# A clustered-attention and SiLU kernel: the hand-written opening list reordered, loads of later batches issued at other steps, output quarters placed in other PSUM banks

## The chip, the core and the metric

The kernel runs on one core of a Trainium2 chip. A core has five engines with queues of their own: TensorE (PE, with its weight loads shown as PEld), VectorE (DVE), ScalarE (ACT), GpSimd (POOL) and SyncE (SP), which here only issues DMAs. An engine takes its queue strictly in the order in which the program lists it. TensorE writes into PSUM, of which this kernel uses eight banks: four single ones, numbered 0 to 3, and two pairs for the scores. The metric is the device time of one execution in microseconds, as the median of several runs.

## The reference

```python
q_n, k_n, c_n = ...                      # each row divided by its norm
q_assign = np.argmax(np.einsum('bhsd,hcd->bhsc', q_n, c_n), axis=-1)
k_assign = np.argmax(np.einsum('bhsd,hcd->bhsc', k_n, c_n), axis=-1)
mask = q_assign[:, :, :, None] == k_assign[:, :, None, :]
scores = np.where(mask, scale * np.matmul(q, k.transpose(0, 1, 3, 2)), -1000000000.0)
attn = ...                               # softmax over the keys
x = np.matmul(attn, v)                   # (4, 8, 768, 64), then to (3072, 512)
h = x @ w_in                             # (3072, 2048)
out = (h * (1.0 / (1.0 + np.exp(-h)))) @ w_out
```

There are 4 batches of 8 heads, 768 rows, 64 columns per head and 16 clusters per head. All inputs and the output are 32-bit floats; the kernel computes with half-precision operands.

## The kernel before

**Tiles.** A job is the rows of one head: 768 keys and 768 queries as twelve blocks of 128 rows (for batch 0 a job `k0` to `k7` holds six key blocks and the first three query blocks of a head; two jobs `x0` and `x1` hold the second halves of the queries of four heads each). The rows arrive in a `raw` tile (eight buffers). They are split into a high and a low half-precision part: `hi` (line 105) multiplies and rounds, on ACT, GpSimd or VectorE, and `lo` (line 117) subtracts on VectorE; both write the tile `hl` (four buffers). A transpose brings them into `ab`: in the opening on TensorE (`tr`, line 134) with an eviction by VectorE or ACT (`ev`, line 146), in the later batches by a transposing DMA (`xpose`). From `ab` TensorE computes the cluster logits (`logits_n`); VectorE takes their maximum (`mx_n`) and compares (`ge_n`), and the one-hot rows so found are turned by TensorE (`cd_mm`, or `ct_mm` for two early jobs), scaled (`cd_ev`) and brought into `ab` by a small DMA on SP. With them in the contracted dimension, the product of queries and keys holds the mask.

**Scores and values.** `units` lists 192 steps: for each batch, half of the queries, group of four heads and head, three pairs of key blocks. A step is two score matmuls (`qk_mm`, line 303, into one of two pairs of banks) and one exponential on ACT (`exp`, line 316). Six steps give two heads; then `pv` (line 324) multiplies with the values, `norm` divides, and the result goes transposed into `xt`, by TensorE (`xn_t`, `xn_ev`) or by DMA (`xn_d`). Values are loaded by SP (`load_v`, line 253, five buffers) and cast by GpSimd (`cast_v`, line 258).

**The two dense layers.** When all heads of a batch half stand in `xt`, sixteen up-projections `unit_a` (four matmuls each, then a tanh on ACT and a product on VectorE) fill `gt`; then three row blocks of the output follow, each of four quarters `part_b` (line 425, four matmuls of 512 columns). A row block collects in one PSUM bank, which VectorE evicts (line 437) and SP stores. Batch halves follow one another; while the steps of one are computed, the dense layers of the one before fill TensorE.

**Weights.** `w_load` (line 443) issues, on GpSimd's queue, eight loads of w_in (0 to 7) and four of w_out (8 to 11); the latter are held back by a small copy that waits for an exponential.

**The opening** runs up to step 24 in an order written out by hand, the string `plan` (line 602). Each word is one operation of `first` (line 521): `hi2.P` is the split of job 2 on GpSimd; `xh0`, `xl0` are `hi`, `lo` of job `x0`; `xp0`, `xq0` its two transposes, `xu0`, `xw0` their evictions, `xL0`, `xM0` its logits, `xm0`, `xg0`, `xc0`, `xe0` the steps to its one-hot rows. `qk9`, `ex9` are the scores and the exponential of step 9; `ce3` evicts the one-hot rows of job 3 and issues the DMA that I call `cd3`. `pa1`, `pb1`, `pc1` are the three thirds of the value product of the second pair of heads, `px3`, `py3` the two heads of the last pair; `nm`, `pt`, `pe` normalise, transpose and evict. `a0`, `e0` begin and end an up-projection (three matmuls and the last one); `w0` to `w9` are weight loads, `vl`, `v` a value load and its cast; `j2` are two filler matmuls and `fill(11)` at the start eleven. A digit behind a dot names the PSUM bank.

**After the opening** a loop runs over the steps from 24 on. `at` holds what a step does beside its scores: `put` places the loads, splits, transposes and logits of job i around a step p, which is 32, 35, 39, ... for batch 1 and five steps apart later (made odd). `take` (line 661) fills TensorE: each step adds 1.46 of credit less its own cost, and as long as credit is positive it takes the next `unit_a` (0.66) or `part_b` (0.87). A quarter may be taken only while `gap` is positive and, until a new batch half is five steps away, only while more than five quarters are left (`HOLD`). The three banks 0 to 2 go round in a list `free`; each user takes the first and returns it when its eviction is listed. Bank 3 serves the output quarters.

Of the kernel before, what the change touches and what calls it, by code (L numbers as in the profile page):

```python
# [28 lines left out]
def kernel(  # L29
# [11 lines left out]
    B, H, S, D = q.shape  # L41
# [21 lines left out]
    free, where = [0, 1, 2], {}  # L63
# [214 lines left out]
    jobs = {}  # L278
# [11 lines left out]
    for i in range(H, B * H):  # L290
        h = i % H
# [165 lines left out]
    def fill(n, bk=3):  # L457
        if n:
            junk = bank("junk", n=bk)
            for _ in range(n):  # L460
                nc.tensor.matmul(junk, zz[:, 0:128], zz, start=True, stop=True)
# [10 lines left out]
    nc.vector.memset(ones, 1.0)  # L472
    for vt in vtb:
        nc.vector.memset(vt[:, :, D : D + 1], 1.0)
    fill(11)
    nc.gpsimd.memset(hf, 0.5)
    chl = mp.tile([128, 4, D], f16, name="chl")
    nc.gpsimd.memset(chl[:, 3, :], 0.0)
# [42 lines left out]
    def first(op, n, eng, banks):  # L521
        job = jobs.get(n)
        xj = jobs["x", n] if n < 2 else None
        if op == "j":
            fill(n, banks[0])
        elif op == "hi":
            for part in (K, Qp) if n == 0 else (None,):
                hi(job, {"A": "act", "P": "pool", "D": None}[eng], part)
        elif op == "lo":
            for part in (K, Qp) if n == 0 else (None,):  # L530
                lo(job, part=part)
        elif op == "tr":
            tr(job, banks)
        elif op in ("evk", "evq"):
            ev(job, op[2], eng)
        elif op == "L":
            logits_n(job, banks[0])
        elif op == "mx":
            mx_n(job)
        elif op == "ge":  # L540
            ge_n(job)
        elif op == "cm":
            cd_mm(job)
        elif op == "ce":
            cd_ev(job, eng)
        elif op == "ct":
            ct_mm(job, banks)
        elif op == "ctq":
            ct_q(job)
        elif op == "ctk":  # L550
            ct_k(job)
        elif op == "qk":
            qk_mm(n)
        elif op == "ex":
            exp(n)
        elif op == "vl":
            load_v(n)
        elif op == "v":
            cast_v(n)
        elif op == "w":  # L560
            w_load(n, {8: 22, 9: 23}.get(n))
        elif op in ("pa", "pb", "pc"):
            t = "abc".index(op[1])
            pv(2 * n, 0, banks and banks[0], [(t, 0), (t, 1)])
        elif op in ("px", "py"):
            pv(2 * n, 0, banks and banks[0], [(t, "xy".index(op[1])) for t in range(NM)])
        elif op == "a":
            begun[n] = unit_a_begin(0, 0, n)
        elif op == "e":
            unit_a_end(0, 0, n, begun.pop(n) if n in begun else unit_a_begin(0, 0, n))()  # L570
        elif op == "nm":
            norm(2 * n, 0)
        elif op == "pt":
            xn_t(2 * n, 0, banks[0])
        elif op == "pe":
            xn_ev(2 * n, 0, eng)
        elif op == "xr":
            load(xj)
        elif op == "xh":
            hi(xj, {"P": "pool", "D": None}[eng])  # L580
        elif op == "xl":
            lo(xj)
        elif op == "xt":
            xpose(xj)
        elif op in ("xp", "xq"):
            tr(xj, banks, "k" if op == "xp" else "q")
        elif op in ("xu", "xw"):
            ev(xj, "k" if op == "xu" else "q", eng)
        elif op in ("xL", "xM"):
            logits_n(xj, banks and banks[0], ns=range(6) if op == "xL" else range(6, 12))  # L590
        elif op == "xm":
            mx_n(xj)
        elif op == "xg":
            ge_n(xj)
        elif op == "xc":
            cd_mm(xj)
        elif op == "xe":
            cd_ev(xj, eng)
        else:
            raise ValueError(op)  # L600

    plan = """
        hi0.A lo0 tr0.32 hi2.P j2.1 evk0.D evq0.A c5.01 j2.2 stk hi1.A L0.3 lo2 j1.2 kad xr0
        mx0 tr2.02 hi3.P ge0 j1.1 lo1 j1.1 evk2.A evq2.D ct0.10 hi4.P lo3 vl1 vl0 xr1 L2.2 ctq0 ctk0 tr1.31 mx2 hi5.P
        qk0 evk1.D evq1.A vl2 ex0 tr3.01 ge2 lo4 cm2 hi6.P L1.3 evk3.A ce2.D qk1 vl4 evq3.A mx1 tr4.02 ex1 ge1
        L3.1 hi7.P evk4.D evq4.A qk2 mx3 ct1.02 ex2 ge3 v1 lo5 cm3 ctq1 L4.3 v0 ce3.A ctk1 w0 tr5.01 mx4 v2
        qk3 ge4 evk5.A w1 evq5.D qk4 lo6 cm4 ex3 j2.2 ce4.D vl3 ex4 v4 qk5 lo7 L5.2 ex5 qk6 mx5 tr6.10 ex6 ge5 qk7
        xh0.P evk6.D cm5 ex7 qk8 ce5.D tr7.31 evq6.D ex8 qk9 evk7.D L6.2 vl5 ex9 w2 evq7.D qk10 mx6 v3 L7.0 ex10
        ge6 qk11 cm6 ex11 pa0.3 ce6.D pb0 mx7 qk12 w3 ge7 ex12 v5 qk13 pc0 cm7 ex13 nm0 ce7.D qk14 ex14 xl0 xh1.P qk15 xp0.1 pt0.3 qk16 pe0.D xu0.D xq0.2 xw0.D
        ex15 vl6 w4 ex16 qk17 pa1.0 vl7 xL0.2 qk18 pb1 ex17 w5 xM0 xm0 xg0 qk19 pc1 xc0 ex18 nm1 xe0.D qk20 w6 v6 pa2.1 ex19  # L610
        pt1.0 qk21 pb2 ex20 pe1.D xl1 w7 v7 qk22 pc2 xp1.2 ex21 nm2 xu1.D qk23 xq1.0 px3.3 ex22 pt2.1 xw1.D ex23 w8 pe2.D xL1.2 xM1 xm1 xg1 a0 py3 nm3 xc1 a1 w9 pt3.3 pe3.D xe1.D e0 e1 qk24 ex24 e2
    """.split()
    for word in plan:
        name, *rest = word.split(".")
# [8 lines left out]
        else:  # L623
            op = name.rstrip("0123456789")
# [5 lines left out]
    def put(s, f, *a):  # L630
        at.setdefault(s, []).append((f, a))
# [3 lines left out]
    for i in range(H, B * H):  # L635
        b, h = divmod(i, H)
        p = int((32 + 3.5 * h, 64 + 5 * h, 104 + 5 * h)[b - 1]) | 1
        job = jobs[i]
        e = 1 if b == 1 else 2
        put(p - 8 - 2 * (b > 1), load, job)  # L640
        put(p - 6, load_v, i)
        put(p - 3 * e, hi, job)
        put(p - 1 - e, lo, job)
        put(p - e, xpose, job)
        put(p, cast_v, i)
        put(p + 5, logits_1, job)
        put(p + 5, lsum, job)
        put(p + 5, mx_n, job)
        put(p + 5, ge_n, job)
        put(p + 7, cd_mm, job)  # L650
        put(p + 7, cd_ev, job, "D")
# [3 lines left out]
    qa, qb = [(0, 0, fb) for fb in range(3, NFB)], []  # L655
# [5 lines left out]
    def take(hold, held):  # L661
        nonlocal turn, gap
        b_ok = len(qb) > hold and gap > 0
        if qa and not (b_ok and (held or turn >= 4)):
            turn = (turn + 1) % 7
            gap += 1
            it = qa.pop(0)
            while not free:
                late.pop(0)()
            late.append(unit_a(*it))  # L670
            if it[2] == NFB - 1:
                qb.extend((it[0], it[1], t, n) for t in range(NM) for n in range(4))
            return 0.66
        if b_ok:
            turn = (turn + 1) % 7
            f = part_b(*qb.pop(0))
            if f:
                late.append(f)
                gap = -1
            return 0.87  # L680
        return 0.0

# [135 lines left out]
```

## Time and profile before

| what | value |
|---|---|
| median of 3 runs | 324.86 us (323.74 to 325.95) |
| profiled execution | 326.72 us, of which the span is 324.9 us |
| mean granted TensorE clock | 0.989 |
| HBM read and written | 27.30 MB and 6.29 MB |
| largest groups on TensorE | up-projection 91.2 us, scores 92.2 us, output 89.2 us, value product 41.5 us |
| exponentials on ACT | 192 of 811 ns, 152.6 us |

The span is the time from the first to the last instruction of one profiled execution; the rest of that execution lies around it. A group's busy time adds up its instructions; matmuls overlap in the pipeline, so the groups' sum is larger than the time that TensorE was busy. In a row of the timeline stand the start, the duration, the engine, the line and the operation, the tile written and the tiles read, shapes and count, and in brackets how long the engine stood idle before and what released it.

### The profile page before, as it was taken

Reading aid. Unit: us, or ns where it says so; the run is one execution under the profiler, and the core shown is the slowest. Engines: PE = TensorE matmul, PEld = TensorE weight load, DVE = VectorE, ACT = ScalarE, POOL = GpSimd, SP = SyncE. Lnnn points to the kernel's source line nnn. Section 1 sums busy time; section 2 is a strip of 40 time slices with the busy share of each in tenths; the row PEclk is TensorE's granted clock in tenths of the full one; section 3 lists DMA queues with packets and bytes.
Section 4 is the critical chain, followed back from the end, with each engine's and each line's share of the span. In section 5 each row is a group of like instructions: output and inputs, shape, how many; then the busy total and the mean of one; then the engine's idle time right before and its main releaser. Section 6 shows DMA issues by size and latency. Waiting matters only on the chain.

```text
span 324.9 us, 7844 instructions
## 1 busy us (share of the span) xinstructions
PE 307.2 (95%) x3173; PEld 191.3 (59%) x3173; DVE 211.7 (65%) x445; ACT 209.4 (64%) x332; POOL 41.0 (13%) x68
## 2 busy tenths in 40 slices
PE   6997999997989999999999999999999999999995
PEld 2665765655556555665566656666566556655644
DVE  5897566779778655987598857893456315632641
ACT  2597649766468665885488656985589648961620
POOL 4884331101000000000010002000000000000000
PEclk9899899999999999999999999999999999999999
DMA  7756999999945686677887567853110111011001
GB/s 218 248 108 132 168 148 253 184 241 206 247 120 135 162 184 186 150 161 132 237 186 185 128 171 210 138 115 83 53 46 12 37 54 46 6 42 46 32 32 68
DMA packets 72613, 43.14 MB, mean 133 GB/s; under 512 B 50016, under 2 KB 68608, under 8 KB 72576
## 3 DMA queue, kind: packets, MB, share of 16 engines
q1 hardware_dynamic: 69024, 38.14, 47.3%
q0 software_dynamic: 3264, 4.20, 8.6%
q8 instruction: 25, 0.41, 0.5%
q10 hardware_dynamic: 288, 0.30, 0.3%
q14 instruction: 12, 0.10, 0.1%
HBM read 27.30 MB, written 6.29 MB: 103 GB/s over the span
## 4 chain that ended last, share of the span: by engine, by line
PE 74%; DVE 14%; ACT 3%; DMA 3%; issue 2%; SPq 2%; POOL 0%; DVEq 0%; ACTq 0%
PE po L430 23%; PE ph L380 20%; PE pS L313 13%; PE pO L330 9%; PE psN L168 3%; DVE hl L120 3%; DVE gt L400 2%; ACT tn L399 2%; DVE ot L437 2%; PE phs L410 2%; ACT P L318 2%; DVE mxn L193 2%; DMA ab<-hl 1%; PE po L782 1%; DVE L L180 1%
## 5 line engine op out<-in xcount | busy, mean ns | idle before, releaser
L318 ACT ACTIVATE P<-pS 128x768 f16<-128x768 f32 x192 | 152.6, 811 | 67.2 <-PE pS L313 67.0
L380 PE MATMUL ph<-xt,win_s 128*128 128x384 f16 x480 | 91.2, 326 | 3.2 <-DVE gt L400 1.7
L313 PE MATMUL pS<-ab 128*128 128x384 f16 x384 | 92.2, 328 | 0.7 <-ACT P L318 0.6
L430 PE MATMUL po<-wout_s,gt 128*128 128x512 f16 x368 | 89.2, 379 | 1.6 <-DVE ot L437 0.9
L400 DVE SCALAR_TENSOR_TENSOR gt<-tn,ph 128x384 f16<-128x384 f32 x120 | 64.0, 551 | 24.3 <-ACT tn L399 23.8
L399 ACT ACTIVATE tn<-ph 128x384 f32<-128x384 f32 x120 | 58.8, 496 | 15.9 <-PE ph L380 11.7
L380 PEld LDWEIGHTS <-win_s 128*128 128x128 f16 x480 | 45.8, 98 | 33.3 <-issue 4.7
L430 PEld LDWEIGHTS <-gt 128*128 128x128 f16 x368 | 34.5, 98 | 37.0 <-issue 3.4
L313 PEld LDWEIGHTS <-ab 128*128 128x128 f16 x384 | 34.7, 98 | 25.5 <-issue 1.7
L330 PEld LDWEIGHTS <-P 128*128 128x128 f16 x1152 | 40.3, 98 | 5.3 <-issue 0.7
L330 PE MATMUL pO<-vt,P 128*128 128x65 f16 x1152 | 41.5, 193 | 0.0
L260 POOL CAST vt<-vn 128x384 f16<-128x384 f32 x32 | 17.0, 533 | 157.5 <-DMA vn<-in_v_dram 127.5
L120 DVE SCALAR_TENSOR_TENSOR hl<-raw,hl 128x768 f16<-128x768 f32 (+3 forms) x35 | 33.9, 972 | 0.4 <-POOL hl L113 0.3
L437 DVE TENSOR_SCALAR ot<-po 128x512 f32<-128x512 f32 x23 | 15.8, 689 | 27.5 <-PE po L430 27.1
L168 PEld LDWEIGHTS <-ab 128*128 128x128 f16 x496 | 18.1, 98 | 5.6 <-DMA ab<-hl 1.5
L180 DVE TENSOR_REDUCE L<-psN 128x192 f32<-128x384 f32 x24 | 13.2, 552 | 11.9 <-PE psN L168 11.9
L168 PE MATMUL psN<-stk,ab 128*128 128x32 f16 (+1 forms) x496 | 19.3, 187 | 1.2 <-DMA ab<-hl 1.1
L342 DVE TENSOR_TENSOR xn<-pO,zr 128x384 f16<-128x384 f32 x32 | 17.8, 557 | 1.1
L340 DVE RECIPROCAL zr<-pO 128x6 f32<-128x6 f32 x32 | 6.2, 194 | 15.7 <-PE pO L330 15.7
L224 DVE TENSOR_SCALAR cd<-psC,kadd 96x256 f16<-96x256 f32 x24 | 11.4, 474 | 6.2 <-PE psC L211 6.0
L113 POOL TENSOR_SCALAR hl<-raw 128x576 f16<-128x576 f32 (+1 forms) x8 | 14.4, 1816 | 2.6 <-DMA raw<-in_q_dram 1.7
L115 DVE TENSOR_SCALAR hl<-raw 128x768 f16<-128x768 f32 x24 | 13.4, 560 | 2.0 <-DMA raw<-in_k_dram 1.9
(68 smaller groups left out, 138.8 us busy)
## 6 DMA issues: line engine op xcount, KB each, us to landing
vn<-in_v_dram SPq DMA_DIRECT2D x32, 192.0 KB, 3.1
raw<-in_k_dram SPq DMA_DIRECT2D x31, 192.0 KB, 3.3
out_dram<-ot SPq DMA_DIRECT2D x23, 256.0 KB, 2.3
raw<-in_q_dram SPq DMA_DIRECT2D x24, 192.0 KB, 2.8
win_s<-in_moe_w_in_dram POOLq DMA_DIRECT2D x8, 256.0 KB, 6.3
wout_s<-in_moe_w_out_dram POOLq DMA_DIRECT2D x4, 512.0 KB, 8.7
ab<-cd SPq DMA_DIRECT2D x26, 48.0 KB, 2.3
raw<-in_q_dram SPq DMA_DIRECT2D x2, 384.0 KB, 5.0
```

What stands on the lines that cost most here:

```text
L120: nc.vector.scalar_tensor_tensor(out=hl[:, s, 1, :], in0=raws[job.name][:, s, :], scalar=QS, in1=hl[:, s, 0, :], op0=ALU.mult, op1=ALU.sub ...
L168: nc.tensor.matmul(L[:, n % 2, :, n // 2], ab[:, i, :], stk[:, job.groups[i // 3][0], x : x + w], start=(x == 0), stop=(x + w == 2 * HC),)
L260: nc.gpsimd.tensor_copy(vt[:, :, 0:D], vns.pop(i))
L313: nc.tensor.matmul(pS[:, e, 0:HALF], abs_[kj.name][:, kn, :], rhs, start=True, stop=True)
L318: nc.scalar.activation(out=P, in_=pst.pop(u)[:, :, 0:HALF], func=AF.Exp, bias=0.0, scale=ESC)
L330: nc.tensor.matmul(o[:, (2 * t + h) * VW : (2 * t + h + 1) * VW], Ps[i + h, c, j // 2][:, j % 2, ts(t, 128)], vtb[(i + h) % 13][:, j, 0:VW ...
L342: nc.vector.tensor_tensor(out=xn, in0=ov[:, :, 0:D], in1=zr.unsqueeze(2).to_broadcast([128, 2 * NM, D]), op=ALU.mult)
L380: nc.tensor.matmul(ph[:, 0:HALF], win_s[:, r, ts(fb, 128)], xts[b, c][:, r, :], start=(r == 0), stop=(r == NR - 1))
L399: nc.scalar.activation(out=tn, in_=ph[:, 0:HALF], func=AF.Tanh, bias=0.0, scale=0.5)
L400: nc.vector.scalar_tensor_tensor(out=gt[:, fb, :], in0=tn, scalar=1.0, in1=ph[:, 0:HALF], op0=ALU.add, op1=ALU.mult)
L430: nc.tensor.matmul(po, gts[b, c][:, fc, ts(t, 128)], wout_s[:, fc, :], start=(fc == 0), stop=(fc == NFB - 1))
L437: nc.vector.tensor_scalar(out=ot, in0=po, scalar1=0.5, scalar2=None, op0=ALU.mult)
```

## The change

The change touches the opening list, the steps at which later loads are issued, and the bank and spacing of the output quarters. No instruction that computes is removed; two filler matmuls are added (`fill(13)`).

In the list, `w0`, `w1`, `w2` now stand right behind the splits `hi5`, `hi6`, `hi7` on GpSimd's queue and the other loads of w_in follow sooner. `vl3` and `vl5` are issued earlier on SP, each one `ce` sooner. `xl0` moves ahead of `ce7` and `nm0`; `xh1` is listed later, but on GpSimd's own queue it still follows the last load of w_in. `xp0` stands ahead of step 15's scores, `pt0` behind `xq0`. `py3` comes ahead of `xm1`, so `nm3` and `pt3` come sooner and `a0`, `a1` around them later. The rows of the first job of batch 1 (`r8`) are loaded inside the list.

In the loop, the rows of batch 1 are loaded 8 to 12 steps ahead of p (8 before), those of batches 2 and 3 16 steps ahead (10 before). When no up-projection is left, an output row block may start in any bank of `free`, and the quarters of the next one are not barred for two steps.

```diff
-    fill(11)
+    fill(13)
...
+        elif op == "r":
+            load(jobs[n])
...
-        mx0 tr2.02 hi3.P ge0 j1.1 lo1 j1.1 evk2.A evq2.D ct0.10 hi4.P lo3 vl1 vl0 xr1 L2.2 ctq0 ctk0 tr1.31 mx2 hi5.P
-        qk0 evk1.D evq1.A vl2 ex0 tr3.01 ge2 lo4 cm2 hi6.P L1.3 evk3.A ce2.D qk1 vl4 evq3.A mx1 tr4.02 ex1 ge1
-        L3.1 hi7.P evk4.D evq4.A qk2 mx3 ct1.02 ex2 ge3 v1 lo5 cm3 ctq1 L4.3 v0 ce3.A ctk1 w0 tr5.01 mx4 v2
-        qk3 ge4 evk5.A w1 evq5.D qk4 lo6 cm4 ex3 j2.2 ce4.D vl3 ex4 v4 qk5 lo7 L5.2 ex5 qk6 mx5 tr6.10 ex6 ge5 qk7
-        xh0.P evk6.D cm5 ex7 qk8 ce5.D tr7.31 evq6.D ex8 qk9 evk7.D L6.2 vl5 ex9 w2 evq7.D qk10 mx6 v3 L7.0 ex10
-        ge6 qk11 cm6 ex11 pa0.3 ce6.D pb0 mx7 qk12 w3 ge7 ex12 v5 qk13 pc0 cm7 ex13 nm0 ce7.D qk14 ex14 xl0 xh1.P qk15 xp0.1 pt0.3 qk16 pe0.D xu0.D xq0.2 xw0.D
-        ex15 vl6 w4 ex16 qk17 pa1.0 vl7 xL0.2 qk18 pb1 ex17 w5 xM0 xm0 xg0 qk19 pc1 xc0 ex18 nm1 xe0.D qk20 w6 v6 pa2.1 ex19
-        pt1.0 qk21 pb2 ex20 pe1.D xl1 w7 v7 qk22 pc2 xp1.2 ex21 nm2 xu1.D qk23 xq1.0 px3.3 ex22 pt2.1 xw1.D ex23 w8 pe2.D xL1.2 xM1 xm1 xg1 a0 py3 nm3 xc1 a1 w9 pt3.3 pe3.D xe1.D e0 e1 qk24 ex24 e2
+        mx0 tr2.02 hi3.P ge0 j1.1 lo1 j1.1 evk2.A evq2.D ct0.10 hi4.P lo3 vl1 vl0 xr1 L2.2 ctq0 ctk0 tr1.31 mx2 hi5.P w0
+        qk0 evk1.D evq1.A vl2 ex0 tr3.01 ge2 lo4 cm2 hi6.P w1 L1.3 evk3.A ce2.D qk1 vl4 evq3.A mx1 tr4.02 ex1 ge1
+        L3.1 hi7.P w2 evk4.D evq4.A qk2 mx3 ct1.02 ex2 ge3 v1 lo5 cm3 ctq1 L4.3 v0 w3 ce3.A ctk1 tr5.01 mx4 v2 vl3
+        qk3 ge4 evk5.A evq5.D qk4 lo6 cm4 w4 ex3 j2.2 ce4.D vl5 ex4 v4 qk5 lo7 L5.2 ex5 qk6 mx5 tr6.10 ex6 ge5 qk7
+        xh0.P w5 evk6.D cm5 ex7 qk8 ce5.D tr7.31 evq6.D ex8 qk9 evk7.D L6.2 v3 ex9 w6 evq7.D qk10 mx6 v5 L7.0 ex10
+        ge6 qk11 cm6 ex11 pa0.3 ce6.D pb0 mx7 qk12 w7 ge7 ex12 qk13 pc0 cm7 xl0 ex13 ce7.D vl6 vl7 r8 qk14 nm0 ex14 xp0.1 qk15 xu0.D xq0.2
+        ex15 qk16 xw0.D pt0.3 ex16 pa1.0 pe0.D qk17 xL0.2 ex17 xh1.P pb1 qk18 xM0 xm0 xg0 ex18 pc1 qk19 xc0 nm1 xe0.D v6 v7 ex19
+        pa2.1 qk20 pt1.0 pb2 ex20 pe1.D qk21 pc2 xl1 ex21 nm2 xp1.2 qk22 xu1.D ex22 xq1.0 px3.3 qk23 xw1.D pt2.1 pe2.D ex23 w8 xL1.2 xM1 py3
+        xm1 xg1 nm3 a0 xc1 pt3.3 a1 w9 pe3.D xe1.D e0 e1 qk24 ex24 e2
...
-        put(p - 8 - 2 * (b > 1), load, job)
+        if i > H:
+            put(p - (8 + min(h, 4) if b == 1 else 16), load, job)
...
-            f = part_b(*qb.pop(0))
+            f = part_b(*qb.pop(0), None if not qa and free else 3)
             if f:
                 late.append(f)
-                gap = -1
+                gap = -1 if qa else 1
```

## The prediction

> **What bounds the kernel now.** I read the engine totals of the page first, then busy time in windows, then the timeline wherever TensorE stands idle.
>
> ```profile
> span 324.9 us, 7844 instructions
> PE 307.2 (95%) x3173; PEld 191.3 (59%) x3173; DVE 211.7 (65%) x445; ACT 209.4 (64%) x332; POOL 41.0 (13%) x68
> 50.00:60.00 10.00, 10.00 (x92) 6.30 (x90) 7.70 (x15) 9.11 (x18) 1.75 (x4) 1.00 1.06 220
> 70.00:80.00 10.00, 7.56 (x114) 4.73 (x111) 9.76 (x20) 7.16 (x11) 1.44 (x3) 1.00 0.96 231
> ```
>
> A window's columns are its length, busy time of PE, weight loads, DVE, ACT and POOL, then granted clock, DMA share, GB/s. TensorE is the bound: from 50 to 60 us it never stops. What can be won is its idle time, 324.9 - 307.2 = 17.7 us, and time at a lowered clock. The lowered clock comes next, in windows laid on its edges.
>
> ```profile
> 4.41:7.82 3.41, 1.59 (x14) 0.72 (x13) 2.91 (x10) 0.23 (x1) 1.72 (x2) 1.00 0.91 272
> 7.82:11.24 3.42, 3.42 (x37) 2.04 (x35) 2.05 (x5) 1.50 (x4) 3.42 (x3) 0.50 0.97 305
> 28.30:31.71 3.41, 1.74 (x20) 0.87 (x18) 2.70 (x5) 2.91 (x4) 3.10 (x4) 1.00 0.45 79
> 31.71:35.13 3.42, 3.36 (x28) 2.69 (x29) 1.38 (x4) 1.01 (x2) 3.42 (x7) 0.50 0.97 201
> 76.09:79.50 3.41, 2.28 (x24) 1.19 (x22) 3.38 (x7) 1.75 (x3) 0.00 (x0) 1.00 1.18 222
> ```
>
> The clock falls to one half for 3.4 us after each window of that length in which TensorE was busy for only 1.59 or 1.74 us; after one with 2.28 us it did not. The second dip falls on work that is all on the path: 3.42 / 2 = 1.71 us lost.
>
> ```profile
> 27.98 0.33 DVE L202 TENSOR_TENSOR om<-psN,mxn 128x160 f16<-128x160 f32 x1
> 29.16 0.48 PE L313 MATMUL pS<-ab 128*128 128x384 f16 x2
> 29.69 0.47 DVE L224 TENSOR_SCALAR cd<-psN,kadd 80x256 f16<-80x256 f32 x1
> 30.07 2.13 POOL L113 TENSOR_SCALAR hl<-raw 128x768 f16<-128x768 f32 x1
> 30.08 1.63 DVE L120 SCALAR_TENSOR_TENSOR hl<-raw,hl 128x768 f16<-128x768 f32 x1
> 31.77 0.82 PE L143 MATMUL pTk<-ident,hl 128*128 128x128 f16 x6 [1.43 <-DVE hl L120]
> 39.00 0.95 DVE L120 SCALAR_TENSOR_TENSOR hl<-raw,hl 128x768 f16<-128x768 f32 x1
> ```
>
> This is its cause. `xp0` (31.77) stands in TensorE's queue and waits for `xl0` (30.08), which stands on VectorE behind `nm0` and `ce7` (29.69) and runs beside GpSimd's `xh1`, 1.63 us against 0.95 alone.
>
> **The split in front of `xp0`.** The new list puts `xl0` right after `ge7`, which ends at 27.98 + 0.33 = 28.31. Alone it ends at 29.26, beside a GpSimd split at 29.94. `xp0`, now behind `qk14` (29.16, two matmuls of 0.16 us), could start at 29.5. So the gap of 1.43 us goes, or all but 0.45 us of it. The window 28.30 to 31.71 then holds some 1.2 us more work, 2.9 us in place of 1.74, more than the 2.28 that kept the clock, so the 1.71 us go too.
>
> The TensorE page of the Trainium skill ("TensorE: Matmul & The Clock Gate", Part 1 and the closing table) says that activity windows of 3413 ns run freely and advises against idle gaps above about 3 us. The window's length agrees with the rows; the gap of 1.43 us that sufficed here is shorter, so by that advice the dip has another cause and 1.71 us of my sum stay lost.
>
> **The end of the list.** `py3` now comes before `a0`, so `nm3` runs sooner, and `a1` goes behind `pt3`.
>
> ```profile
> 44.41 0.34 PE L352 MATMUL px<-ident,xn 128*128 128x128 f16 x3 [0.27 <-DVE xn L342]
> 45.20 0.48 PE L380 MATMUL ph<-xt,win_s 128*128 128x384 f16 x2 [0.45 <-DVE xt L363]
> 45.53 0.49 PE L313 MATMUL pS<-ab 128*128 128x384 f16 x2
> ```
>
> The two waits, 0.27 + 0.45 = 0.72 us, are covered by `a1`. Against them stand three places where TensorE's next item hangs on VectorE: `xc0` behind `xg0`, `xp1` behind `xl1` (now ahead of `nm2`), `pt3` behind `nm3`, with `a1`, `e0` and `qk24` queued behind it. Each is bounded by 0 and 0.45 (the longer wait above); I take 0.2, in all 0.6. Opening: 1.43 + 1.71 + 0.72 - 0.6 = 3.26, say **3.2 us**; step 24 (`qk24`, 45.53) starts near 42.3.
>
> **GpSimd and the DMAs of w_in.** Eight w_in issues move forward, three between splits.
>
> ```profile
> 14.23 3.26 POOL L113 TENSOR_SCALAR hl<-raw 128x576 f16<-128x576 f32 x2 [0.79 <-PE pTq L143]
> 17.45 0.96 POOL L260 CAST vt<-vn 128x384 f16<-128x384 f32 x2
> 18.34 0.75 POOL L449 DMA_DIRECT2D win_s<-in_moe_w_in_dram  x1
> 22.33 0.74 DVE L120 SCALAR_TENSOR_TENSOR hl<-raw,hl 128x576 f16<-128x576 f32 x1
> 27.04 0.89 PE L330 MATMUL pO<-vt,P 128*128 128x65 f16 x24
> 28.61 0.50 POOL L260 CAST vt<-vn 128x384 f16<-128x384 f32 x1 [5.38 <-DMA vn<-in_v_dram]
> ```
>
> An issue holds GpSimd for up to 0.75 us. The first fills the 0.79 us in which it waits anyway; two more delay `hi7` (ending 17.49) and the first casts (18.41) by at most 1.5 us. Their users come at 22.33 and 27.04, so this costs nothing; without that cover it would be 1.5 us. The later casts wait for their value loads (28.61), which SP now issues sooner.
>
> What could suffer is a load beside the w_in stream, `cd3` first:
>
> ```profile
> 19.49 3.50 SPq L226 DMA_DIRECT2D ab<-cd  x2
> 24.69 0.49 PE L313 MATMUL pS<-ab 128*128 128x384 f16 x2
> DMA to landing us min/median/max: 5.1/5.1/5.1
> DMA to landing us min/median/max: 2.2/2.3/5.1
> DMA to landing us min/median/max: 2.6/3.1/9.2
> ```
>
> The landing rows are, in order, that of the `cd3` DMA alone, of all `cd` DMAs, and of all value loads. `cd3` left at 19.49 and landed at 24.6, just ahead of `qk9` (24.69) that needs it. It already ran beside w_in then (issues at 18.34 and 19.55), at the slowest landing of its kind, so I take no change; the bounds are 2.2 and 9.2, a gain that the queue ahead of `qk9` absorbs and a stall of 4.0.
>
> **Two more fill matmuls.**
>
> ```profile
> 1.18 4.13 PE L461 MATMUL junk<-zz 128*128 128x512 f16 x11 [1.18 <-DVE zz L471]
> 6.90 0.51 PE L143 MATMUL pTk<-ident,hl 128*128 128x128 f16 x6 [1.59 <-DVE hl L120]
> ```
>
> Eleven take 4.13, so two end by 6.06, inside the gap before 6.90: no cost. The window 4.41 to 7.82 rises from 1.59 to at most 2.34 busy, between what lost the clock and what kept it. If it keeps it, the first 3.4 us of real work run faster, but that stretch hangs on VectorE's splits and holds five filler matmuls. Between 0 and 0.9 I take **0.3 us**.
>
> **The step loop.** A step gains 1.46 of credit less its fixed cost (0.33 for its scores), held at 2.0; an output quarter costs 0.87; while credit is positive the next item is taken. Before, the fourth quarter of a row block barred quarters for two steps, since bank 3 had to be emptied; now, with no up-projection left, it bars none. Worked through: the loads and scores of steps 24 to 34 are as before; step 35 takes two quarters in place of one, 36 one, and 37 none in place of two. At step 47 credit is at its cap of 2.0: before, one quarter ended a row block and barred step 48, and three came in step 49; now three come in step 47 and one in 48.
>
> ```profile
> 78.84 0.52 PE L168 MATMUL psN<-stk,ab 128*128 128x32 f16 x12 [1.13 <-DMA ab<-hl]
> 80.62 2.75 PE L430 MATMUL po<-wout_s,gt 128*128 128x512 f16 x12
> 59.28 0.86 PE po L430 x4
> ```
>
> The 12 matmuls at 80.62 are those three quarters of step 49, and 78.84 is step 48's logits, which waited 1.13 us for a transposed operand. With two quarters (2 x 0.86 = 1.72 us) moved ahead, they come later than the operand lands: up to 1.13 won. VectorE, busy 9.76 of 10 us there, may show behind it; I take **0.8 us**.
>
> ```profile
> 120.55 0.56 DVE L115 TENSOR_SCALAR hl<-raw 128x768 f16<-128x768 f32 x1 [1.22 <-DMA raw<-in_k_dram]
> 122.46 2.75 PE L430 MATMUL po<-wout_s,gt 128*128 128x512 f16 x12 [0.87 <-DVE ot L437]
> ```
>
> At step 75 a new row block waited 0.87 us for bank 3, whose eviction stood on VectorE behind a split that waited 1.22 us for rows of batch 2. Both ends of that go: the rows are issued 16 steps ahead in place of 10, and the block takes another bank. Of 0.87 I take **0.8 us**. On SP these loads move past transposes and stores and wait for a `raw` buffer only; the queue's other items keep their order.
>
> Against it: an output block left unfinished from step 35 to 47 now holds one of the three free banks, so pO, px, psN and psC rotate over two. Most of them need the eviction of the bank that they get anyway; I count three waits of 0.1 us (bounds 0 and 0.87, the bank wait above): **-0.3 us**.
>
> Sum: 3.2 + 0.3 + 0.8 + 0.8 - 0.3 = **4.8 us**. The profiled execution took 326.72 us (span 324.9 and 1.8 around it) and would take 321.9. It lies 0.6% above the median of the three runs, 324.86, so I forecast 324.86 - 4.8 = **320.1 us**.
>
> **The rivals.** *The overlap stays* (0.16): GpSimd's queue does not know the list's place of `xh1`; if its value loads land early, `xh1` runs beside `xl0`, 0.68 us longer, the window stays near 2.3 busy and the clock still falls. 0.68 + 1.71 = 2.4 fewer: 322.5. For it speaks the row of 1.63; against it that `xl0` moves ahead by 1.77 us and `xh1` waits for the cast at 28.61.
>
> *The split is shut out altogether* (0.05): with `xh1` ahead of it, `xl0` would start when its 2.13 us end, and end at 28.31 + 2.13 + 0.95 = 31.4; of gap and dip, 1.1 + 1.71 return: 322.9. The SBUF page of the Trainium skill ("SBUF — State Buffer", Who interferes with whom) has this as a rule: a VectorE instruction with two SBUF inputs and a GpSimd one that reads SBUF exclude each other. The row at 30.08 agrees in part only: 1.63, not the 3.1 of full exclusion.
>
> *The dip has another cause* (0.07): 4.8 - 1.71 = 3.1: 321.8. *The two-bank rotation costs* 0.87 at each of three stretches in place of 0.3 in all (0.06): 2.3 fewer, 322.4. *The change does nothing of it* (0.04): new waits take the place of all, 324.9.
>
> *The w_in stream starves the small loads* (0.09): with eight w_in loads queued from 14 us on, `cd3` lands in 9.2 us as the slowest value load did, at 28.7. `qk9` heads TensorE's queue, all else stands behind it: 4.0 us, and a window more than half idle costs a dip of 1.71. 324.86 - 4.8 + 5.7 = 325.8, slower than before; with a second dip 327.5. It decides from a landing of 5.1 + 4.8 - 1.71 = 8.2 us on. For it: 5.1 against a median of 2.3. Against it: w_in ran beside it before.
>
> **The numbers.** The forecast has 0.53. Its own range: all terms at their better bound (1.43 + 1.71 + 0.72 + 0.9 + 1.13 + 0.87 = 6.8) give 318.1; the opening at its worse one (0.98 + 1.71 + 0.72 - 3 x 0.45 = 2.1), without the 0.3 of the fill, gives 2.1 + 0.8 + 0.8 - 0.3 = 3.4, 321.5. Taking in the rivals up to 325.8 leaves out about 0.06 below and 0.08 above: 318.0 to 325.8. Three runs spread over 0.7%, so about 1% can be told from no change. Faster by over 1% means below 321.6: most of the forecast's 0.53 and some of the neighbours, 0.58; slower, above 328.1, only the last rival with more on top, 0.08; the rest, 0.34.
>
> **What would show it.** Right: in the new profile `xp0` starts by 30.3 us without a wait for `hl`, the clock stays at 1.00 from 28 to 36 us, `qk24` starts near 42.3, and the waits of 1.13 at the logits and 0.87 at `po` are gone. Wrong: `qk9`, `qk12` or `qk15` idle behind `ab`; `xl0` at 1.6 us; a new half-clock window; `psN` or `pO` waiting for evictions between steps 37 and 48.

## The result, and the profile after

The changed kernel takes 322.93 us (median of 10 runs, 321.36 to 324.35) where the kernel before takes 324.44 (10 runs, 323.51 to 325.95). The ratio is 0.9946 with a 95% interval of 0.9922 to 0.9969: 0.0054 x 324.44 = 1.75 us less. The forecast was 4.8 us less. The time lies within the range given, near several rivals' times, but no rival's mechanism accounts for it. Step 24 came when forecast, though not by the terms of the sum, and the kernel before is usually faster than its profiled execution showed.

First the page and the timeline of the changed kernel, TensorE's rows (start, duration, engine, line, operation, tiles, and in brackets the idle time before and its releaser).

```profile
span 321.6 us, 7853 instructions
...
PE 305.5 (95%) x3175; PEld 190.2 (59%) x3175; DVE 209.7 (65%) x445; ACT 210.7 (66%) x332; POOL 47.9 (15%) x68
```

```profile
28.16 0.51 PE L143 MATMUL pTk<-ident,hl 128*128 128x128 f16 x6 [0.15 <-DVE hl L120]
29.23 0.50 PE L313 MATMUL pS<-ab 128*128 128x384 f16 x2 [0.56 <-DMA ab<-cd]
...
32.74 0.50 PE L313 MATMUL pS<-ab 128*128 128x384 f16 x2 [0.48 <-DMA ab<-cd]
...
42.46 0.49 PE L313 MATMUL pS<-ab 128*128 128x384 f16 x2
...
71.64 0.52 PE L168 MATMUL psN<-stk,ab 128*128 128x32 f16 x12 [0.67 <-DVE xn L342]
...
104.90 1.02 PE L430 MATMUL po<-wout_s,gt 128*128 128x512 f16 x4 [0.66 <-DVE gt L400]
```

`xp0` starts at 28.16 where it stood at 31.77, and step 24 (42.46) starts where the forecast put it, near 42.3 (how it got there is told below). The waits of 1.13 at step 48's logits and 0.87 at a row block are gone, and four new ones have come: `qk15` (29.23) and `qk18` (32.74) behind one-hot rows that a DMA brings into `ab`, the logits at 71.64 behind the eviction of a shared bank, and a row block at 104.90 behind the product of an up-projection, whose bank it now takes.

VectorE's timeline and the windows of the same kernel (length, busy PE, weight loads, DVE, ACT, POOL, then clock, DMA share, GB/s):

```profile
26.17 0.48 DVE L224 TENSOR_SCALAR cd<-psN,kadd 80x256 f16<-80x256 f32 x1 [1.15 <-DMA ab<-cd]
...
27.16 0.95 DVE L120 SCALAR_TENSOR_TENSOR hl<-raw,hl 128x768 f16<-128x768 f32 x1
...
29.28 0.48 DVE L224 TENSOR_SCALAR cd<-psN,kadd 80x256 f16<-80x256 f32 x1 [1.17 <-DMA ab<-cd]
```

```profile
28.30:31.71 3.41, 2.73 (x45) 1.86 (x43) 2.33 (x6) 2.18 (x4) 2.78 (x3) 1.00 0.88 123
31.71:35.13 3.42, 2.80 (x63) 2.08 (x60) 1.50 (x5) 2.35 (x3) 0.00 (x0) 1.00 1.02 194
```

In this profile `xl0` takes 0.95 (at 27.16) and not 1.63, the window holds 2.73 busy, and the clock stays at 1.00. What has grown is VectorE's waiting in front of the evictions of one-hot rows, 1.15 and 1.17 us (nothing in the first profile of before, 1.1 us in all in its second): the tile `cd` has two buffers, and the DMA that empties one of them had not landed.

### The profile page after: what moved, and what is told of

It is laid out like the page before. It is cut to its first block, busy times and chain, and to the rows that moved or that the text cites. A ratio compares the mean times of both kernels' runs of the same rounds, so it can differ in the third digit from the quotient of the medians.

```text
span 321.6 us, 7853 instructions
## 1 busy us (share of the span) xinstructions
PE 305.5 (95%) x3175; PEld 190.2 (59%) x3175; DVE 209.7 (65%) x445; ACT 210.7 (66%) x332; POOL 47.9 (15%) x68
## 4 chain that ended last, share of the span: by engine, by line
PE 72%; DVE 14%; DMA 5%; ACT 4%; issue 3%; POOL 1%; SPq 1%; DVEq 0%; ACTq 0%; POOLq 0%
PE po L430 24%; PE ph L380 19%; PE pS L313 14%; PE pO L330 9%; DMA ab<-cd 3%; DVE gt L400 3%; ACT P L318 2%; DVE hl L120 2%; PE psN L168 2%; DVE mxn L193 2%; ACT tn L399 2%; PE phs L410 2%; DVE L L180 1%; DMA raw<-in_q_dram 1%; DVE om L202 1%
## 5 line engine op out<-in xcount | busy, mean ns | idle before, releaser
L430 PE MATMUL po<-wout_s,gt 128*128 128x512 f16 x368 | 90.2, 379 | 0.7 <-DVE gt L400 0.7
L260 POOL CAST vt<-vn 128x384 f16<-128x384 f32 x32 | 22.5, 706 | 153.1 <-DMA vn<-in_v_dram 127.8
L120 DVE SCALAR_TENSOR_TENSOR hl<-raw,hl 128x768 f16<-128x768 f32 (+3 forms) x35 | 32.4, 928 | 0.8 <-POOL hl L113 0.7
L113 POOL TENSOR_SCALAR hl<-raw 128x576 f16<-128x576 f32 (+1 forms) x8 | 15.7, 1966 | 2.2 <-DMA raw<-in_q_dram 2.1
L193 DVE TENSOR_REDUCE mxn<-L 128x12 f32<-128x192 f32 x24 | 12.0, 500 | 0.8
```

The source lines that it names most:

```text
L120: nc.vector.scalar_tensor_tensor(out=hl[:, s, 1, :], in0=raws[job.name][:, s, :], scalar=QS, in1=hl[:, s, 0, :], op0=ALU.mult, op1=ALU.sub ...
L193: nc.vector.tensor_reduce(out=mx[:, 0 : 2 * m].rearrange("p (h m) -> p h m", h=2), in_=Ls[job.name].rearrange("p h c m -> p h m c"), axis= ...
L260: nc.gpsimd.tensor_copy(vt[:, :, 0:D], vns.pop(i))
L430: nc.tensor.matmul(po, gts[b, c][:, fc, ts(t, 128)], wout_s[:, fc, :], start=(fc == 0), stop=(fc == NFB - 1))
```

## The experiments

Each kernel was timed in 8 to 12 runs beside the kernel before, and the ratios are to that kernel on the same chip; kernels of one group shared a chip.

| kernel | ratio | 95% interval | median us |
|---|---|---|---|
| group 1: kernel before, as it is (`a1_control`) | 1.0023 | 1.0001 to 1.0045 | 325.20 |
| opening alone (`a2_opening`) | 0.9967 | 0.9950 to 0.9983 | 323.44 |
| loop alone (`a3_loop`) | 0.9960 | 0.9944 to 0.9976 | 323.06 |
| `fill(13)` alone (`a4_fill`) | 0.9988 | 0.9969 to 1.0007 | 324.06 |
| group 2: later loads alone (`b3_loads`) | 1.0005 | 0.9989 to 1.0020 | 324.05 |
| bank rule alone (`b4_banks`) | 0.9986 | 0.9970 to 1.0002 | 323.21 |
| change, four `cd` buffers (`b2_cd4`) | 0.9945 | 0.9926 to 0.9964 | 321.91 |
| change, w_in at old places (`b5_wold`) | 0.9973 | 0.9951 to 0.9996 | 323.03 |
| group 3: change again (`c1_after`) | 0.9945 | 0.9922 to 0.9968 | 322.07 |
| change, both of the two edits above (`c2_wold_cd4`) | 0.9960 | 0.9938 to 0.9982 | 322.39 |
| change, four `cd` buffers, banks alternating (`c3_cd4_alt`) | 0.9926 | 0.9901 to 0.9951 | 321.71 |
| change without the bank rule (`c4_bank3`) | 0.9956 | 0.9931 to 0.9981 | 322.52 |

The identical kernel came out at 1.0023 of itself with an interval that just leaves out 1, so differences of 0.2% are not to be read as effects. The profiles say more: from step 24 on, the same code gives the same stretch to a few hundredths of a microsecond in several profiles. The next table is worked out from the timelines of all fourteen: a step starts with the first of its two score matmuls; the first three columns are such starts, the others differences of two of them (the last one up to the end of the span).

| kernel | step 0 | step 14 | step 24 | 24 to 52 | 52 to 190 | 190 to end |
|---|---|---|---|---|---|---|
| before, first profile | 13.98 | 29.16 | 45.53 | 38.99 | 207.72 | 32.71 |
| before, second profile (`a1_control`) | 13.75 | 28.83 | 43.39 | 38.38 | 207.58 | 32.70 |
| loop alone | 13.81 | 29.12 | 43.64 | 38.12 | 207.19 | 33.31 |
| `fill(13)` alone | 12.75 | 28.34 | 42.62 | 38.43 | 207.58 | 32.70 |
| later loads alone | 12.69 | 28.27 | 43.35 | 39.35 | 207.07 | 32.74 |
| bank rule alone | 12.67 | 28.29 | 43.21 | 37.82 | 207.16 | 33.27 |
| changed, first profile | 12.85 | 27.52 | 42.46 | 38.60 | 207.19 | 33.31 |
| changed, second profile (`c1_after`) | 12.85 | 29.33 | 43.58 | 37.77 | 207.50 | 33.31 |
| opening alone | 12.56 | 27.24 | 42.36 | 38.57 | 208.32 | 32.72 |
| change, four `cd` buffers | 12.83 | 27.51 | 41.77 | 37.77 | 207.17 | 33.31 |
| banks alternating | 12.54 | 27.22 | 41.90 | 37.86 | 206.89 | 33.30 |
| without the bank rule | 12.76 | 27.41 | 41.99 | 38.90 | 206.87 | 32.74 |
| change, w_in at old places | 12.77 | 27.97 | 41.05 | 37.78 | 207.15 | 33.30 |
| both edits (`c2_wold_cd4`) | 12.68 | 28.27 | 42.23 | 37.77 | 207.17 | 33.28 |

**The kernel before, once more.** No edit.

> The kernel before, unchanged, as a control. Theory 1 (the half-clock stretches come and go): its profiled execution had two of them (mean clock 0.989), most others have fewer; the list of executions shows clocks up to 0.995 and more, and each stretch fewer shortens the span by 0.8 to 1.7 us, so that spans run from 321.5 to 325. Theory 2 (the stretches are always there and the loop gave the gain back): the clock stays near 0.989 in nearly all executions, and spans do not follow it.

Its second profile, in this order: cores, TensorE's timeline, VectorE's, GpSimd's, and the windows on the edges where the first profile showed the half clock.

```profile
core 0: 322.0 us, clock 0.998
```

```profile
30.76 0.51 PE L143 MATMUL pTk<-ident,hl 128*128 128x128 f16 x6 [0.74 <-DVE hl L120]
...
43.39 0.48 PE L313 MATMUL pS<-ab 128*128 128x384 f16 x2
...
76.10 0.52 PE L168 MATMUL psN<-stk,ab 128*128 128x32 f16 x12 [0.47 <-DMA ab<-hl]
...
119.56 2.75 PE L430 MATMUL po<-wout_s,gt 128*128 128x512 f16 x12 [0.77 <-DVE ot L437]
```

```profile
29.76 0.94 DVE L120 SCALAR_TENSOR_TENSOR hl<-raw,hl 128x768 f16<-128x768 f32 x1
```

```profile
31.05 2.12 POOL L113 TENSOR_SCALAR hl<-raw 128x768 f16<-128x768 f32 x1
```

```profile
28.30:31.71 3.41, 2.37 (x31) 1.44 (x27) 2.24 (x5) 2.59 (x4) 2.98 (x4) 1.00 0.42 66
31.71:35.13 3.42, 3.25 (x74) 2.64 (x71) 1.85 (x6) 2.76 (x4) 3.42 (x5) 1.00 0.78 182
```

The same program, unaltered, has no half-clock stretch in these windows; GpSimd's split starts at 31.05 in place of 30.07, so `xl0` runs without it, in 0.94; the gap in front of `xp0` is 0.74 in place of 1.43, and step 24 starts 2.14 us sooner (43.39 against 45.53). Nearly all of that lies in steps 14 to 18: 4.28 us in place of 6.38. How often the dip comes is told by the granted clocks of the executions of the kernel before: in the three groups there are 107, and 98 of them have a mean clock of 0.997 or more. Nine lie between 0.992 and 0.995, none at the 0.989 of the first profile. Two stretches of 3.41 us at half clock lower the mean of a 324.9 us span by 2 x 1.71 / 324.9 = 0.0105, which is what 0.989 lacks; one lowers it to 0.995 (the control's 0.998 comes from a last stretch at half clock, from 321.05 to its end). Where in those nine the stretch lay was not recorded. They took 0.3 to 3.0 us longer than the median of the others in their group, in the middle 1.8. So a price of 1.71 for a dip fits, while its presence belonged to one execution and not to the kernel. Of the 88 executions with the new list on record, 4 have such a clock too (0.992 to 0.995).

The clock column doesn't show every slow stretch. Two filler matmuls ahead of step 0, in the control and in the profile of the later loads alone, the same code up to there:

```profile
7.96 1.06 PE L461 MATMUL junk<-zz 128*128 128x512 f16 x2
```

```profile
7.82 0.59 PE L461 MATMUL junk<-zz 128*128 128x512 f16 x2
```

The column reads 1.00 for both. Of the five profiles with `fill(11)`, three have such a slow stretch in their start and reach step 0 at 13.75 to 13.98, two at 12.67 and 12.69; the nine with `fill(13)` all reach it at 12.54 to 12.85.

**The opening alone, and two filler matmuls alone.**

```diff
-    fill(11)
+    fill(13)
...
+        elif op == "r":
+            load(jobs[n])
...
-        put(p - 8 - 2 * (b > 1), load, job)
+        if i > H:
+            put(p - 8 - 2 * (b > 1), load, job)
```

To this the opening has the new list in full; `a4_fill` has only the first hunk.

> Only the opening of the change (list and fill of 13, first rows of batch 1 in the list); loads of later batches and output quarters as before. Theory 1: 1.3 to 2.0 us less than before, as much as the whole change, ratio 0.994 to 0.996. Theory 2: 3 us less, ratio 0.990 to 0.991, since the opening gained 3.06 us in the profile and only the loop took it back.

> Only thirteen fill matmuls in place of eleven. Theory 1: 0 to 0.4 us less in the median, since the first half-clock stretch goes only in the executions that had it; ratio 0.998 to 1.000. Theory 2: 0.8 us less (the lead that the changed kernel had in the profile at its fifth step), ratio 0.9975.

The opening gives 0.9967, 0.0033 x 324.38 = 1.07 us, where the forecast had 3.2 + 0.3 and the two theories 0.994 to 0.996 and 0.990 to 0.991: less than any of them. Its step 24 starts at 42.36, like that of the whole change. Two filler matmuls alone give 0.9988 with 1 inside the interval; on the median their 0.3 us can't be told from nothing, though step 0 starts about 1 us sooner than in the profiles with a slow start.

**The loop alone, and its two parts.** `a3_loop` has both hunks, `b3_loads` the first, `b4_banks` the others.

```diff
-        put(p - 8 - 2 * (b > 1), load, job)
+        put(p - (8 + min(h, 4) if b == 1 else 16), load, job)
...
-            f = part_b(*qb.pop(0))
+            f = part_b(*qb.pop(0), None if not qa and free else 3)
...
-                gap = -1
+                gap = -1 if qa else 1
```

> Only the loop of the change (loads further ahead, output quarters in any free bank, no barred steps); opening as before. Theory 1: no change to 0.4 us more, ratio 0.999 to 1.002, the removed waits of 1.13 and 0.87 us replaced by new ones. Theory 2: 1.5 us more, ratio 1.004 to 1.005. My forecast had 1.3 us less, ratio 0.996.

> The kernel before with the later loads alone: rows of batch 1 issued 8 to 12 steps ahead, of batches 2 and 3 16 steps. The loop alone measured 0.996, 1.3 us less. If the loads carry it: 0.9955 to 0.9975 here, the wait of 0.87 us for bank 3 behind the late rows gone in most executions, and some variation of the spans with it. If the free banks carry it: 0.999 to 1.001.

> The kernel before with the output quarters in any free bank and no barred steps, loads as before. If the banks carry the loop's gain: 0.9955 to 0.9975, since the logits of step 48 no longer wait for the transposed rows (1.13 us). If the loads carry it: 0.999 to 1.002, since the profile of the changed kernel shows new waits of 0.67 and 0.66 us in place of that one.

The timeline of the later loads alone, of the bank rule alone, and of the change without the bank rule:

```profile
77.03 0.52 PE L168 MATMUL psN<-stk,ab 128*128 128x32 f16 x12 [1.08 <-DMA ab<-hl]
```

```profile
104.85 1.02 PE L430 MATMUL po<-wout_s,gt 128*128 128x512 f16 x4 [0.66 <-DVE gt L400]
```

```profile
75.21 0.52 PE L168 MATMUL psN<-stk,ab 128*128 128x32 f16 x12 [1.06 <-DMA ab<-hl]
```

Without the bank rule the logits of step 48 wait again (1.08 and 1.06); with it they don't wait for that operand, and steps 24 to 52 take 37.8 us in most profiles, in place of 38.4 to 39.4. The wait of a row block for bank 3 (0.77 to 1.50 in the four profiles with neither part) is gone with either part: steps 52 to 190 take 207.07 and 207.16 against 207.58. But the bank rule brings the 0.66 at 104.85, and it lengthens the end from step 190 on by 0.6 us, in all profiles with it. Where that comes from stands in VectorE's timeline, first of the kernel before, then of the changed one, and in TensorE's of the changed one:

```profile
294.11 0.56 DVE L342 TENSOR_TENSOR xn<-pO,zr 128x384 f16<-128x384 f32 x1
296.64 0.36 DVE L363 COPY xt<-px 128x384 f16<-128x384 f16 x1 [1.97 <-PE px L352]
297.50 0.69 DVE L437 TENSOR_SCALAR ot<-po 128x512 f32<-128x512 f32 x1 [0.51 <-PE po L430]
```

```profile
294.75 0.56 DVE L342 TENSOR_TENSOR xn<-pO,zr 128x384 f16<-128x384 f32 x1
296.24 0.69 DVE L437 TENSOR_SCALAR ot<-po 128x512 f32<-128x512 f32 x1 [0.94 <-PE po L430]
296.85 0.35 DVE L363 COPY xt<-px 128x384 f16<-128x384 f16 x1
```

```profile
296.21 0.65 PE L410 MATMUL phs<-xt,win_s 128*128 128x384 f16 x3
297.25 0.97 PE L410 MATMUL phs<-xt,win_s 128*128 128x384 f16 x5 [0.39 <-DVE xt L363]
```

The quarters now end a row block just ahead of the last `xt`, so its eviction (`ot`, 0.69) runs ahead of the copy to `xt` (296.24, 296.85), and TensorE waits 0.39 for the last up-projections; the rest of the 0.6 was not traced. Before, the eviction came behind it. By the profiles the loop's gain is thus 0.6 + 0.4 - 0.6 = 0.4 us for both parts (37.77, 207.17, 33.28 of the both-edits kernel against 38.38, 207.58, 32.70).

By the runs, the loop alone gives 0.0040 x 324.38 = 1.3 us, its parts 0.45 and -0.16 (0.0014 and -0.0005 of 323.94); the theory that the loop gives its gain back (0.999 to 1.002) fell. The later loads alone (1.0005) thus show no gain, and the bank rule alone (0.9986) lies between what the two theories gave it. The parts, timed on another chip, don't add up to the whole. Opening and loop, 1.07 + 1.3, are more than the 1.75 of the whole change, but within the intervals they agree with it. From step 24 to the end the profile of the loop alone takes 278.62 us, against 278.66 and 279.42 in the two of before (the sums of their three columns). What the loop is worth on the median, between 0.4 and 1.3, stays open.

**The two new waits of the opening.** `b2_cd4` takes VectorE's wait away, `b5_wold` takes w_in's loads off their new places, `c2_wold_cd4` does both.

```diff
-        cd = mp.tile([6 * HC, 256], f16, name="cd", bufs=2)
+        cd = mp.tile([6 * HC, 256], f16, name="cd", bufs=4)
...
-        mx0 tr2.02 hi3.P ge0 j1.1 lo1 j1.1 evk2.A evq2.D ct0.10 hi4.P lo3 vl1 vl0 xr1 L2.2 ctq0 ctk0 tr1.31 mx2 hi5.P w0
+        mx0 tr2.02 hi3.P ge0 j1.1 lo1 j1.1 evk2.A evq2.D ct0.10 hi4.P lo3 vl1 vl0 xr1 L2.2 ctq0 ctk0 tr1.31 mx2 hi5.P
...
-        ex15 qk16 xw0.D pt0.3 ex16 pa1.0 pe0.D qk17 xL0.2 ex17 xh1.P pb1 qk18 xM0 xm0 xg0 ex18 pc1 qk19 xc0 nm1 xe0.D v6 v7 ex19
+        ex15 qk16 xw0.D pt0.3 ex16 pa1.0 pe0.D qk17 xL0.2 ex17 xh1.P w4 w5 pb1 qk18 xM0 xm0 xg0 ex18 pc1 qk19 xc0 nm1 xe0.D w6 v6 w7 v7 ex19
```

In the second of these edits `w0` to `w7` and the casts between them stand about where they stood before the change.

> The changed kernel with four buffers in place of two for the one-hot rows on their way to the small DMA. In its profile VectorE waited 1.15 and 1.17 us for such a buffer in the opening. If that wait is on the path: 0.3 to 0.6 us less than the changed kernel, ratio to the kernel before 0.9925 to 0.9935. If only the landing counts, for which the scores of steps 15 and 18 wait anyway: no change against it, 0.994 to 0.995.

> The changed kernel with the eight loads of w_in back at their old places on GpSimd's queue (three behind the last splits no longer), all else as changed. If the w_in stream delays the small DMAs for which the scores of steps 15 and 18 wait (0.56 and 0.48 us in the profile of the changed kernel, 1.3 us in that of the opening alone): 0.6 to 1.0 us less than the changed kernel, ratio 0.991 to 0.9925. If the small DMAs are as late without it: 0.994 to 0.996.

> The changed kernel with the eight loads of w_in issued at their old places and with four buffers for the one-hot rows in place of two. Theory (the two new waits of the opening, TensorE behind late one-hot DMAs and VectorE behind a buffer held by such a DMA, are what the opening list gives back): both waits are gone, steps 14 to 24 take about 1.5 us less than in the changed kernel, and the time is 1.0 to 1.5 us below it. Rival (these waits are covered, since what follows waits for later weights or evictions anyway): within 0.5 us of the changed kernel on the same chip.

How long the small one-hot DMAs of the opening (18 to 36 us) take to land, from the view of one line's instructions: before, changed (with those that waited), changed again, and with both edits.

```profile
DMA to landing us min/median/max: 2.2/3.4/5.1
```

```profile
  DVE cd L224: 2.3, 2
...
  PE pS L313: 1.0, 2
...
DMA to landing us min/median/max: 2.6/5.6/6.0
```

```profile
DMA to landing us min/median/max: 3.9/5.7/6.9
```

```profile
DMA to landing us min/median/max: 3.8/4.5/6.3
```

Their median is 3.4 to 4.2 in the six profiles with the old list, 4.2 and 4.5 with the new list and w_in at its old places, and 4.7 to 5.7 in the six with w_in ahead. So moving w_in ahead does slow them, by about 1 us in the middle, and TensorE waits for them, 1.0 in one profile of the changed kernel and 1.8 in the other. In that other one it is `qk9` that waits, for `cd3`, which landed in 6.4, and `xl0` runs beside `xh1` (TensorE, VectorE, GpSimd of `c1_after`):

```profile
24.84 0.50 PE L313 MATMUL pS<-ab 128*128 128x384 f16 x2 [1.59 <-DMA ab<-cd]
...
30.68 0.51 PE L143 MATMUL pTk<-ident,hl 128*128 128x128 f16 x6 [0.86 <-DVE hl L120]
```

```profile
28.61 2.00 DVE L120 SCALAR_TENSOR_TENSOR hl<-raw,hl 128x768 f16<-128x768 f32 x1
```

```profile
28.96 2.14 POOL L113 TENSOR_SCALAR hl<-raw 128x768 f16<-128x768 f32 x1
```

Four buffers alone give 0.9945, the ratio of the changed kernel, so taking VectorE's wait away shows no gain. w_in at its old places alone gives 0.9973, worse than both forecasts of its run. With both edits these waits are gone, and steps 14 to 18 take 3.50 us in place of 5.21. But the time didn't follow: 322.39 against 322.07 for the change on the same chip. The table of waits of both edits shows a new one in their place, for casts of values, which now queue behind the later loads of w_in on GpSimd:

```profile
PE pO L330 <- POOL vt L260: 0.7, 2, 0.4
```

Steps 20 to 24 take 8.32 there against 7.58 (both worked out from the starts). The larger part is lost earlier: from step 0 to 14 this kernel takes 15.59 and the changed one 14.68. The pair that differs in w_in alone shows how, `b5_wold` first and then the changed kernel, `lo6` on VectorE and `xh0` on GpSimd:

```profile
19.36 1.44 DVE L120 SCALAR_TENSOR_TENSOR hl<-raw,hl 128x576 f16<-128x576 f32 x1
```

```profile
19.35 2.13 POOL L113 TENSOR_SCALAR hl<-raw 128x768 f16<-128x768 f32 x1
```

```profile
19.45 1.03 DVE L120 SCALAR_TENSOR_TENSOR hl<-raw,hl 128x576 f16<-128x576 f32 x1
```

```profile
23.82 2.13 POOL L113 TENSOR_SCALAR hl<-raw 128x768 f16<-128x768 f32 x1
```

With five w_in loads listed ahead of `xh0` in place of two, it starts only when VectorE's splits are done. Step 8 starts 0.56 behind step 7 in all six profiles with w_in ahead, and 0.88 to 1.47 behind it in the eight others. So the place of w_in trades late one-hot rows against VectorE's splits and late values, and no place of the two tried is better by the runs; my theory that 1.0 to 1.5 us lay in these waits fell. The single profile with w_in at its old places, step 24 at 41.05, was the fastest of its 12 executions (321.14 to 324.82, median 323.03): the second case here in which one profile looked unlike the median.

**The change again, banks alternating, and without the bank rule.** The alternation, on top of four `cd` buffers (`last` starts at 3):

```diff
-            f = part_b(*qb.pop(0), None if not qa and free else 3)
+            bk = None if not qa and free and last == 3 else 3
+            if qb[0][3] == 0:
+                last = bk
+            f = part_b(*qb.pop(0), bk)
```

> The changed kernel again, unaltered, beside three variants on the same chip. If the gain is a property of the kernel, the ratio to the kernel before is 0.9946 within its interval again (0.992 to 0.997), some 1.7 us. The theory that the half-clock stretch was a rare event of one profiled execution says that this ratio stays near 0.995 here too, and not 0.985 as the forecast of 4.8 us would have it.

> The changed kernel with four buffers for the one-hot rows, and with output blocks alternating between bank 3 and a free bank when no up-projection is left, where the changed kernel never uses bank 3 then. Theory (the loop gives back through the three shared banks: 0.67 us at psN and 0.66 us at po in its profile): both waits fall below 0.3 us, and the time is 0.5 to 1.0 us below that of four buffers alone (0.9945 of the kernel before, so 0.991 to 0.993). Rival (the bank waits are covered by later ones): no difference from 0.9945 beyond 0.15%.

> The changed kernel with the bank rule and the spacing of output quarters undone: the new opening and the later loads issued further ahead stay. Theory (the loop's gain needs the bank rule; the loads alone gave nothing): as the opening alone, 0.9967 of the kernel before, within 0.2%, and the 1.13 us at the logits of step 48 is back. Rival (the loads carry it): 0.9946 as the whole change.

`c4_bank3` undoes the hunks of `b4_banks`. The change gives 0.9945 again. With the alternating banks the row block that waited 0.66 starts without a wait, in TensorE's timeline of that kernel:

```profile
103.08 1.02 PE L430 MATMUL po<-wout_s,gt 128*128 128x512 f16 x4
```

Steps 52 to 190 take 206.89, 0.28 less than with the rule as it was in most profiles (207.17), so more than half of the wait was covered. The wait at `psN` is absent too, as in every profile with the bank rule but the changed kernel's first. This kernel has the lowest median (321.71) and ratio (0.9926) of all, as the theory had it, 2.4 us (0.0074 x 323.89) below the kernel before; from the changed kernel its interval does not part it (0.9901 to 0.9951 against 0.9922 to 0.9968). Without the bank rule the ratio, 0.9956, lies between that of the opening alone and that of the whole change and can't be told from either.

## Why the prediction was wrong

**The step that failed** is the last one of the sum: "It lies 0.6% above the median of the three runs, 324.86, so I forecast 324.86 - 4.8 = 320.1 us". The 4.8 held terms that were there only because this execution lay above the median: the dip, 1.71, and half of the gap, 0.69 of 1.43. Its step 24 came at 45.53; the five other profiles with the old list have it at 43.39, 43.35, 43.21, 42.62 and 43.64 (the control, loads alone, banks alone, filler alone, loop alone), in the mean at 43.24. Of that difference, 2.29, about 2.0 lie in steps 14 to 18, where dip and gap stand: 6.38 in this execution, 4.28 to 4.59 in the five. From the execution's own 326.72 the sum was fair: 326.72 - 4.8 = 321.9, against 322.93 measured. Against the median, 1.71 + 0.69 = 2.4 us were taken off a time that didn't hold them; the execution's excess of 1.86 over it (326.72 - 324.86) was the warning. The range didn't catch it either: both of its ends, from 6.8 and from 3.4, hold the 1.71 in full. The other 2.4 of the sum lie inside the measured interval (1.0 to 2.5), but the next paragraph shows that not all of them were right.

**The opening, 3.2.** Right at its end, and that by luck. In the pair of first profiles step 24 came 3.07 sooner, but 1.64 of it lie ahead of step 14, where the sum had the 0.3 of the fill, and 1.43 behind it, where it had 3.2. Against the five other profiles with the old list, the six with the new list and w_in ahead reach step 14 0.86 sooner in the mean (27.71 against 28.57) and take as long from there to step 24 (14.64 against 14.67); step 24 comes 0.9 sooner (42.34 against 43.24), 1.07 by the runs. Ahead of step 14 the gain lies in front of step 0, where the fill acts, and at step 8, through the later `xh0`, which the forecast didn't have. Behind it, the gap went (0.41 or less is left in five of the six), and so did the 0.45 in front of `a0`; the 0.27 at `pt3` stayed (0.28 to 0.29), `xp1` waited 0.17 to 0.27 in five of the six, near the 0.2 taken for it, and `xc0` not at all; what took the gain back are the waits behind one-hot DMAs, 0.9 to 1.3 us there in five of the six, which the sum put at nothing. With w_in at its old places, steps 14 to 24 take 13.08 and 13.95.

**The rule on the clock.** The rows showed a dip after a gap of 1.43 us; I counted it as a property of the kernel. The Trainium skill ("TensorE: Matmul & The Clock Gate", Part 1) states that the windows run freely, without a reset when the kernel starts, and that the number of slow matmuls at the start changes from run to run. The traces agree: two fillers at 8 us take 1.06 us in one profile and 0.59 in another. The later dip came and went as well, in 9 of 107 executions by their clocks. I used this page only to weigh whether the gap was the cause of the dip, and didn't ask whether the dip would come again.

**The w_in stream.** "This costs nothing" and "I take no change" were wrong for the DMAs behind it: landings rose by about 1 us in the middle. The rival that made this its mechanism named `qk9` behind `cd3`, and in the second profile of the changed kernel just that happened, with a landing of 6.4 in place of 9.2 and a stall of 1.59 in place of 4.0, without a dip; in the first, `qk15` and `qk18` waited. By the runs, taking the stream back is no gain.

**The loop, 0.8 + 0.8 - 0.3.** The two waits went as forecast, but in another profile of the kernel before they were 0.47 and 0.77, not 1.13 and 0.87. The wait of the two-bank rotation came as 0.67 in one profile of the changed kernel and not in the other. Unforeseen were the 0.66 at a row block in a shared bank and the 0.6 at the end. I had followed the credit arithmetic to step 49 and not to the last batch half, where an eviction now runs ahead of the last `xt`.

**The rivals.** The overlap stayed in part. In the first profile of the changed kernel it was gone; in the second `xl0` took 2.00 beside `xh1` and `xp0` waited 0.86, and three more with the new opening have 1.58, 1.58 and 1.77, beside casts of values on GpSimd. But the clock didn't fall there, so the rival's 2.4 didn't follow. The split was never shut out for the whole 3.1. The gap as the cause of the dip is neither shown nor refuted: the window with 1.74 us busy lost the clock and that with 2.37 kept it, but so did one with 1.91 of 3.41 us (116.42 to 119.83 of the opening alone) that holds a gap of 1.50, longer than the 1.43, and one with only 1.56 (3.94 to 7.35 of `c1_after`), behind which two fillers take 0.59. The time near the rivals' forecasts is no evidence for them. That this execution itself was unusual wasn't among the rivals and should have been: 326.72 lay above all three runs shown.

## What to carry over

Before a stall in a profile becomes a term of a forecast, ask whether the median execution has it: if the profiled one lies above the runs, subtract from its own time, or profile the unchanged kernel a second time. A half-clock stretch that only some executions have belongs in the range, not in the sum. A forecast that comes out at its end is to be followed through marks on the way (here steps 0, 14 and 24) before its terms are called right. A reordering that is checked where it was meant to help has also to be followed to the end of the program, where an eviction may come to stand ahead of the last operand.

## What the hardware showed that I had not expected

The half clock came and went with no change to the program: the same program had two half-clock stretches in one execution, and of 107 others 98 have a mean clock of 0.997 or more and none less than 0.992. Windows with 1.56, 1.91 and 2.37 of 3.41 us busy kept the clock, others with 1.59 and 1.74 lost it, so TensorE's busy time alone doesn't tell. The mean clock leaves out a slow start: the control's fillers took 1.06 where 0.59 is usual, at a clock column of 1.00. The VectorE split with two inputs took 1.63 and 2.00 beside a GpSimd split in two profiles and 0.94 in a third, where GpSimd's split started after it was done. And small DMAs on SP's queue took 3.4 to 4.5 us to land in the middle in the opening, 4.7 to 5.7 when the w_in loads on GpSimd's queue were issued earlier beside them.
